# One pool of eight PSUM banks for every product, and the order of all steps rewritten

## The chip, the cores and the metric

The kernel runs on one core of a Trainium2 chip. The metric is the device time of one execution in microseconds (us). Shown are the median of three timed executions and one profiled execution.

## The reference, cut to what matters

Two layers follow each other. The first is causal attention with a decay bias (8 batches, 8 heads, 576 positions, head size 64), the second a mixture of 4 attention experts over the first one's output, with 2 experts chosen for each position.

```python
def _attn_ref(q, k, v, s):                      # (8, 8, 576, 64), s (8, 8, 576)
    scores = scale * np.matmul(q, k.transpose(0, 1, 3, 2))
    cum = np.cumsum(np.maximum(s, 0.0), axis=-1)
    bias = -(cum[:, :, :, None] - cum[:, :, None, :])
    scores = np.where(causal, -1e9, scores + np.minimum(bias, 0.0))
    scores = scores - np.max(scores, axis=-1, keepdims=True)
    attn = np.exp(scores)
    attn = attn / (np.sum(attn, axis=-1, keepdims=True) + 1e-09)
    return np.matmul(attn, v)

def _moe_ref(x, w_gate, wq, wk, wv, wo):        # x (8, 576, 512), 4 experts of 64
    logits = x @ w_gate                         # the two largest are kept and softmaxed: w
    for e in range(E):
        q, k, v = x @ wq[e], x @ wk[e], x @ wv[e]
        # causal softmax attention a of this expert
        ye = a @ v @ wo[e]
        # out += w of expert e (zero where it is not chosen) * ye
```

## The kernel before

The work is cut into pairs: two heads of one batch, or two experts of one batch, are one pair, worked on side by side. There are 50 slots, one for each pair and two without. In the steady part six slots make up one batch: four pairs of heads (phase 1) of batch b and then two pairs of experts (phase 2) of batch b-1. The list of `MIDDLE` that holds for a slot is named by its phase and its number in the batch, (1,0) to (1,3) and then (2,0) and (2,1).

Slot n works on pair n and, ahead or behind, on its neighbours. A step is a closure with a short name, and these are the names that matter here (the slot in which a step stands in the order is written before a colon, `0:s2`):

- `ld`: load of queries and keys of pair n+3 (L357, a DMA on SyncE's queue). `lv`: the values (L367, L368). `hc`: the rows with the running sums (L394 to L401).
- `h0` to `h3` (ACT, L406, L409): high parts of queries and keys of pair n+2. `lq`, `lk`: copies of the high parts for pair n+1 (GpSimd or ACT at the start, DMAs later). `l0` to `l3` (DVE, L441, L446): low parts.
- `m0` to `m5` (TensorE, L466): scores in bf16 for the row maxima, one bank each; m3 to m5 are of pair n+1, m0 to m2 of pair n+2. `M0` to `M5` (DVE, L480): the maximum out of the bank. `cb` (DVE, L499) joins two parts. `mt` (TensorE, L503) transposes the maxima, `mA` (ACT, L507) copies them out, `mq` (DMA, L511) writes them into row 96 of the query tile, where the scores product subtracts them.
- `s0` to `s6` (TensorE, L529, L534): scores of pair n, one bank each; `E0` to `E6` (ACT, L550, L560): exponentials. `d0` to `d3` (GpSimd): causal masks and column sums.
- `v0` to `v7` (TensorE, L625): attention times values of pair n-1, in two banks; `V0`, `V1` (ACT, L639): their copies.
- `a0`, `a1` (TensorE, L675) and `A0`, `A1` (ACT): sums over positions; `r0` to `r4`: their reciprocals, spread through memory by DMAs; `n`, `N`, `o`: normalisation and the split into high and low parts.
- `p`, `P` (TensorE L840, ACT L858, L875, L1000): projections of the second layer and their copies. `t0`, `t1`: transposed gate weights. At the end `x..`, `y..`, `q..`, `z..` finish the last pair, the last output projection and its stores.

TensorE's products are of two kinds by the columns of the array that they take. Scores and projections take it whole (weights of 128 columns, or 64 for a last short tile). The products m and v come as two halves of 64 columns, a as four strips of 32.

The order of the whole program is written out in lists: `FILLING` for slots -2 to 9, `MIDDLE` for slots 10 to 43 (six lists, used again and again), `DRAINING` for 44 to 49. Each engine executes its own instructions in the order in which the lists name them, and SyncE issues the DMAs in that order; between engines semaphores make a step wait for what it reads and for the buffer that it writes. A step listed earlier on another engine delays nobody, a step listed earlier on the same engine does.

PSUM has eight banks, and before the change each belongs to a kind of product: two for m (`mx0`, `mx1`), three for s (`s0` to `s2`, by turns), one for v (`pvp`), and two (`pj0`, `pj1`, by turns, `bank_pj`) for all others. At the very end the output projection borrows `mx0`, `mx1` and `s0`. A product waits until its own kind's bank has been read.

Of the kernel before, what the change touches and what calls it, by code (L numbers as in the profile page):

```python
# [8 lines left out]
F32 = mybir.dt.float32  # L9
# [30 lines left out]
def pieces(kt, q0, q1):  # L40
# [4 lines left out]
    for ci, segs in enumerate(SCHUNKS):  # L45
# [65 lines left out]
    ),  # L111
# [4 lines left out]
    ),  # L116
# [4 lines left out]
    ),  # L121
# [4 lines left out]
    ),  # L126
# [4 lines left out]
    ),  # L131
# [1011 lines left out]
```

## Time and profile before

| | |
|---|---|
| median of 3 timed executions | 699.51 us (697.83 to 701.18) |
| profiled execution, its own time | 699.62 us |
| its span, first to last instruction | 697.9 us |
| TensorE busy | 660.4 us, 95% of the span |
| VectorE (DVE) busy | 559.6 us, 80% |
| ScalarE (ACT) busy | 460.2 us, 66% |
| GpSimd (POOL) busy | 459.8 us, 66% |
| mean granted TensorE clock | 0.994 |

Each row of a busy time is the time in which the engine had at least one instruction under way. Matmuls overlap, so a busy TensorE is not one at its peak: what a product really costs is read from the distance between the start of one matmul and that of the next.

### The profile page before, as it was taken

Reading aid. Unit: us, or ns where it says so; the run is one execution under the profiler, and the core shown is the slowest. Engines: PE = TensorE matmul, PEld = TensorE weight load, DVE = VectorE, ACT = ScalarE, POOL = GpSimd, SP = SyncE. Lnnn points to the kernel's source line nnn. Section 1 sums busy time; section 2 is a strip of 40 time slices with the busy share of each in tenths; the row PEclk is TensorE's granted clock in tenths of the full one; section 3 lists DMA queues with packets and bytes.
Section 4 is the critical chain, followed back from the end, with each engine's and each line's share of the span. In section 5 each row is a group of like instructions: output and inputs, shape, how many; then the busy total and the mean of one; then the engine's idle time right before and its main releaser. Section 6 shows DMA issues by size and latency. Waiting matters only on the chain.

```text
span 697.9 us, 16217 instructions
## 1 busy us (share of the span) xinstructions
PE 660.4 (95%) x5816; PEld 526.4 (75%) x5816; DVE 559.6 (80%) x1478; ACT 460.2 (66%) x971; POOL 459.8 (66%) x611
## 2 busy tenths in 40 slices
PE   1587999999999999999999999999999999999997
PEld 0364578878877788878977878878877788879775
DVE  5588996889889888898779878888789887762983
ACT  6276868676657756767766766776676776566463
POOL 9595677578776568666777667766776578736120
PEclk9999999999999999999999999999999999999999
DMA  3433442445355533566444542655534553431304
GB/s 111 128 95 109 135 126 63 121 123 105 104 129 160 159 92 84 143 182 127 109 121 129 150 123 71 172 141 136 123 81 142 159 123 103 107 98 37 85 9 137
DMA packets 52158, 81.21 MB, mean 116 GB/s; under 512 B 18430, under 2 KB 26622, under 8 KB 52078
## 3 DMA queue, kind: packets, MB, share of 16 engines
q1 hardware_dynamic: 52078, 80.18, 43.9%
q8 instruction: 46, 0.75, 0.4%
q14 instruction: 34, 0.28, 0.1%
HBM read 44.55 MB, written 10.09 MB: 78 GB/s over the span
## 4 chain that ended last, share of the span: by engine, by line
PE 73%; DVE 10%; DMA 7%; ACT 4%; issue 3%; SPq 2%; POOL 1%; DVEq 0%; ACTq 0%; POOLq 0%
PE pq L840 13%; PE pvp L625 13%; PE s L529 10%; PE s L534 9%; PE mx L466 8%; PE po L840 7%; PE pw L840 6%; DVE mx L480 4%; PE sm L675 3%; DMA rb<-rr 2%; ACT p L550 1%; DMA rr<-sr 1%; DVE k L446 1%; PE mt L503 1%; DVE q L441 1%
## 5 line engine op out<-in xcount | busy, mean ns | idle before, releaser
L480 DVE CUSTOM_DVE_ANT_0 mx<-mx,mask 128x512 f32<-128x512 f32 (+7 forms) x480 | 217.7, 469 | 56.9 <-PE mx L466 48.5
L569 POOL TENSOR_SCALAR_AFFINE_SELECT p<-p 128x256 f32<-128x256 f32 (+1 forms) x240 | 124.9, 521 | 136.0 <-ACT p L550 135.5
L550 ACT ACTIVATE p<-s 128x512 f32<-128x512 f32 x288 | 163.8, 588 | 58.9 <-PE s L534 55.7
L529 PE MATMUL s<-q,k 128*128 128x256 f32 (+3 forms) x672 | 177.2, 290 | 1.4 <-ACT p L550 1.2
L534 PE MATMUL s<-q,k 97*128 97x256 f32 (+3 forms) x672 | 163.2, 285 | 4.6 <-DMA q<-mr 4.4
L529 PEld LDWEIGHTS s<-q,k 128*128 128x128 f32 (+1 forms) x672 | 124.2, 185 | 20.9 <-issue 12.6
L591 POOL TENSOR_TENSOR r<-r,p 128x640 f32<-128x640 f32 x92 | 133.3, 1448 | 7.7
L534 PEld LDWEIGHTS s<-q,k 97*128 97x128 f32 (+1 forms) x672 | 123.8, 186 | 7.6 <-DMA q<-mr 6.1
L466 PE MATMUL mx<-k,q 96*64 96x320 bf16 (+7 forms) x960 | 107.1, 303 | 23.1 <-ACT q L406 12.5
L625 PE MATMUL pvp<-p,v 128*64 128x128 f32 (+4 forms) x1024 | 105.1, 338 | 0.5 <-ACT pv L639 0.4
L441 DVE TENSOR_TENSOR q<-raw,q 64x576 fp32r<-64x576 f32 x94 | 84.0, 898 | 13.8 <-ACT q L406 8.6
L446 DVE TENSOR_TENSOR k<-raw,k 64x576 fp32r<-64x576 f32 x94 | 80.5, 865 | 16.3 <-DMA k<-k 14.1
L625 PEld LDWEIGHTS pvp<-p,v 128*64 128x64 f32 x1024 | 66.5, 137 | 29.9 <-issue 2.6
L466 PEld LDWEIGHTS <-q 96*64 96x64 bf16 x960 | 45.9, 111 | 56.7 <-DVE mcol L480 18.3
L840 PE MATMUL pq<-xh,wqkh 128*128 128x288 f32 x256 | 77.1, 301 | 0.0
L840 PE MATMUL pq<-xl,wqkh 128*128 128x288 f32 x256 | 75.7, 296 | 0.2 <-DVE xl L739 0.2
L840 PE MATMUL pq<-xh,wqkl 128*128 128x288 f32 x256 | 75.4, 295 | 0.0
L586 POOL TENSOR_TENSOR r<-p 128x256 f32<-128x256 f32 x46 | 41.3, 897 | 50.9 <-ACT p L550 41.3
L409 ACT ACTIVATE k<-raw 64x576 fp32r<-64x576 f32 x96 | 63.9, 680 | 4.5 <-DMA raw<-in_qk_dram 3.0
L406 ACT ACTIVATE q<-raw 64x576 fp32r<-64x576 f32 x96 | 64.5, 680 | 1.9 <-PE s L534 0.7
L480 DVE DVE_READ_ACCUMULATOR2_ANT mcol<- 128x1 f32 x480 | 63.8, 133 | 1.4
L639 ACT ACTIVATE pv<-pvp 128x256 f32<-128x256 f32 x92 | 37.3, 405 | 39.5 <-PE pvp L625 39.3
(117 smaller groups left out, 1181.8 us busy)
## 6 DMA issues: line engine op xcount, KB each, us to landing
raw<-in_qk_dram SPq DMA_DIRECT2D x30, 576.0 KB
rb<-rr SPq DMA_DIRECT2D x92, 144.0 KB
q<-q SPq DMA_DIRECT2D x45, 288.0 KB
k<-k SPq DMA_DIRECT2D x39, 288.0 KB
v<-in_vm_dram SPq DMA_DIRECT2D x32, 256.0 KB
out_dram<-o SPq DMA_DIRECT2D x32, 256.0 KB
q<-mr SPq DMA_DIRECT2D x96, 2.2 KB
raw<-in_qk_dram SPq DMA_DIRECT2D x4, 288.0 KB
```

The lines of the kernel that those rows point to most:

```text
L406: nc.scalar.activation(q2[0:64, j], get_raw(n, j)[0:64], AF.Copy)
L441: eng.tensor_tensor(a[64:128, j], get_raw(n, j)[0:64], q2[0:64, j].bitcast(F32), op=OP.subtract)
L446: eng.tensor_tensor(c[0:64, j], get_raw(n, j)[64:128], c[64:128, j].bitcast(F32), op=OP.subtract)
L466: nc.tensor.matmul(t[64 * j : 64 * j + 64, c0 : c0 + k1 - k0], q2[0:RC, 64 * qt : 64 * qt + 64], k2[0:RC, k0:k1], start=True, stop=True,)
L480: nc.vector.tensor_tensor_reduce(t[:, c0 : c0 + w], t[:, c0 : c0 + w], mask[:, m0 : m0 + w], scale=1.0, scalar=NEG, op0=OP.add, op1=OP.max ...
L529: nc.tensor.matmul(t[0:nk, c0 : c0 + q1 - q0], K1[r1(n)][:, j, k0 : k0 + nk], Q1[r1(n)][:, j, q0:q1], start=True, stop=False,)
L534: nc.tensor.matmul(t[0:nk, c0 : c0 + q1 - q0], K2[r2(n)][0 : RM + 1, j, k0 : k0 + nk], Q2[r2(n)][0 : RM + 1, j, q0:q1], start=False, stop= ...
L550: nc.scalar.activation(ptile[n][:, x % 2, 512 * ci : 512 * ci + 512], tl[x], AF.Exp, scale=0.125)
L569: nc.gpsimd.affine_select(out=a, in_=a, pattern=[[0, 2], [1, nk]], compare_op=OP.is_ge, fill=0.0, base=0, channel_multiplier=-1,)
L591: add(r[:, :, q0:S], r[:, :, q0:S], p[:, :, 1024 + c : 1024 + c + S - q0], op=OP.add)
L625: nc.tensor.matmul(cur[h][64 * j : 64 * j + 64, q0 - PVC[h] : q1 - PVC[h]], vsl(j, kt), ptile[n][:, j, c : c + q1 - q0], start=first, stop ...
L840: nc.tensor.matmul(t[0:nk, 0:w], l, r, start=(x == 0), stop=(x == len(terms) - 1))
```

## The change

All eight banks go into one queue. `take` hands out the bank at the head of the queue, `give` puts a bank back at its tail when the step that reads it out is listed. Both happen while the program is written, so the lists decide which bank a product gets; on the chip the product waits, as before, until the bank's last reader is done. A bank's last reader is now sometimes ACT and sometimes DVE.

```diff
+    banks = list(range(8))
+    taken = {}
+
+    def take(name):
+        t = ps.tile([P, 512], F32, tag=f"bank{banks[0]}", name=name, bufs=1)
+        taken[id(t)] = t, banks.pop(0)
+        return t
+
+    def give(t):
+        banks.append(taken.pop(id(t))[1])
...
-            mbank[n, bi] = t = ps.tile([P, 512], F32, tag=f"mx{bi % 2}", name=f"mx{n}_{bi}", bufs=1)
+            mbank[n, bi] = t = take(f"mx{n}_{bi}")
...
-            return ps.tile([P, 512], F32, tag=f"s{(x + n) % 3}", name=f"s{n}_{x}", bufs=1)
+            return take(f"s{n}_{x}")
...
-                cur[h] = ps.tile([P, 512], F32, tag="pvp", name=f"pvp{n}_{h}", bufs=1)
+                cur[h] = take(f"pvp{n}_{h}")
...
-        t = bank_pj(name)
+        t = take(name)
...
+                give(t[0])
```

Each copy or reduction that reads a product out ends with a `give` of its bank, and every `bank_pj` becomes a `take`. No instruction is added, removed or resized. All lists are new. Every step keeps its slot and stands elsewhere in the order; the list of slots (1,0), as an example:

```diff
-        "l2 v0 lk m3 v1 M3 s0 hc E0 p0 s2 ld s3 s1 V0 h1 E1 E2 h0 lq h2 P0 p1 s4 s5 l1 m4 M4 E4 "
-        "v2 m5 M5 v3 v4 h3 m2 v5 M2 v6 m1 E3 d1 v7 m0 cb mt P1 mA l3 M1 lv d0 p2 s6 a1 P2 V1 mq "
-        "E5 M0 d2 l0 a0 A0 A1 E6 d3"
+        "v0 m3 v1 s1 s0 l2 hc lq h2 E1 E0 s3 s2 ld p0 P0 p1 s5 h0 M3 E3 V0 h3 m5 M5 h1 m4 M4 v2 "
+        "v4 m2 v3 v5 m0 cb P1 E2 E5 mt p2 s4 M2 mA l0 s6 a0 lv E6 lk l1 mq E4 a1 m1 P2 d1 A1 d2 "
+        "d3 d0 l3 A0 M1 M0 v6 v7 V1"
```

The stretch of `FILLING` up to the first scores, from where the two orders part on SyncE's queue (`...` stands for steps left out; `0:ld` waits until a buffer of pair 0 has been read):

```diff
-    "-1:hc -1:m0 0:ld -1:M3 0:lv -1:mt -1:l0 -1:M0 0:h1 -1:l2 -1:m2 -1:mA -1:m1 0:h2 -1:mq 0:s2 "
...
+    "0:l1 0:l0 -1:hc -1:m2 -1:mA 0:l3 -1:m0 0:m5 -1:mq -1:m1 -1:cu 0:h2 0:h3 -1:l0 -1:l3 -1:l2 "
+    "-1:l1 0:s2 0:s1 -1:M0 0:s3 0:E3 0:s0 0:ld 0:E0 0:m4 -1:M2 0:m3 0:M5 0:lc 0:l2 0:E1 0:M4 "
```

In the new list `-1:ld` and `-1:hc` follow `1:lv` on SyncE's queue, and `0:lv` comes after `0:mq`; on GpSimd `0:lq` comes after `0:lc` and `0:f2`, and on ACT `-1:lk` after the four steps `-2:h`.

More of the change, by code (lines that the diff above doesn't have):

```diff
@@ L484, in reduce @@
                 )
+            give(t)
         for bi in banks:
@@ L501, in turn @@
         def turn():
-            t[0] = bank_pj(f"mt{n}")
+            t[0] = take(f"mt{n}")
             nc.tensor.transpose(t[0][0:9, 0:P], mcol[n][:, 0:9], ident)
@@ L552, in exp @@
             )
+            give(tl[x])
         def tail():
@@ L563, in exp_tail @@
             )
+            give(tl[6])
         def diag(kt):
@@ L639, in copy @@
                 nc.scalar.activation(pvtile[n][:, q], cur[h][:, 0:w], AF.Copy)
+            give(cur[h])
         x = 0
@@ L670, in half @@
         def half(h):
-            t[h] = bank_pj(f"sm{n}_{h}")
+            t[h] = take(f"sm{n}_{h}")
             for x in range(2):
@@ L686, in copy @@
             )
+            give(t[h])
         return {
@@ L751, in sum_up @@
             q0, q1 = LASTQ[k]
-            t[k] = bank_pj(f"sm{m}_{k}")
+            t[k] = take(f"sm{m}_{k}")
             for j in range(2):
@@ L765, in copy @@
             )
+            give(t[k])
         def one_over(k):
@@ L790, in tile_attention_then_moe @@
     ot = {}
-    npj = [0]
-    def bank_pj(name):
-        npj[0] += 1
-        return ps.tile([P, 512], F32, tag=f"pj{npj[0] % 2}", name=name, bufs=1)
     def out_tile(b, tt):
@@ L809, in part @@
             if tt not in t:
-                t[tt] = (
-                    bank_pj(f"po{b}_{tt}") if tt < 2 else
-                    ps.tile([P, 512], F32, tag=("mx0", "mx1", "s0")[tt - 2], name=f"po{b}_{tt}", bufs=1)
-                )
+                t[tt] = take(f"po{b}_{tt}")
             for x, (y, w) in enumerate(((xH, WOH), (xH, WOL), (xL, WOH))):
@@ L822, in copy @@
             nc.scalar.activation(out_tile(b, tt)[0:nk, 0:DM], t[tt][0:nk, 0:DM], AF.Copy)
+            give(t[tt])
         def store(tt):
@@ L858, in copy @@
                 nc.scalar.activation(raw2[b, e // 2][:, e % 2, q], t[0][:, 0:HS], AF.Copy)
+                give(t[0])
             return mm, copy, None
@@ L875, in copy @@
                 nc.scalar.activation(vx[0:nk, tt, :], t[0][0:nk, 0:260], AF.Copy)
+                give(t[0])
             return mm, copy, None
@@ L927, in turn @@
             o, tts = parts[x]
-            t[x] = bank_pj(f"gt{b}_{o}")
+            t[x] = take(f"gt{b}_{o}")
             for tt in tts:
@@ L939, in copy @@
             nc.scalar.activation(t["g4"][:, o : o + w], t[x][0:E, 0:w], AF.Copy)
+            give(t[x])
         def send():
@@ L957, in spread @@
         def spread(i, h):
-            t["k", i, h] = bank_pj(f"gt{b}{i}_{h}")
+            t["k", i, h] = take(f"gt{b}{i}_{h}")
             nc.tensor.matmul(
@@ L969, in keep @@
             )
+            give(t["k", i, h])
         items = {
@@ L1000, in copy @@
                 nc.scalar.activation(t[1][0:nk, 0:DM], t[0][0:nk, 0:DM], AF.Copy)
+                give(t[0])
             def store():
```

159 rows, old and new, of tables (DRAINING, FILLING, MIDDLE) are left out of this document.

## The prediction

> **What bounds the kernel now.** I read the page first: busy times, then the slices.
>
> ```profile
> span 697.9 us, 16217 instructions
> PE 660.4 (95%) x5816; PEld 526.4 (75%) x5816; DVE 559.6 (80%) x1478; ACT 460.2 (66%) x971; POOL 459.8 (66%) x611
> PE   1587999999999999999999999999999999999997
> PEclk9999999999999999999999999999999999999999
> ```
>
> TensorE is busy from the fourth slice to the last but one; only the first 60 us show holes. The profiled execution took 699.62 us, 1.7 us around its span and 0.1 us above the median of 699.51, so terms of the span carry over to the time unchanged. Next, busy times by stretch (TensorE, weight loads, DVE, ACT, POOL, clock, DMA): three of the start, then one full batch of the steady part, from the first scores of slot 17 to those of slot 23.
>
> ```profile
> 20.00:40.00 20.00, 12.60 (x77) 8.94 (x75) 11.32 (x40) 8.29 (x17) 11.92 (x15) 0.95 0.44 127
> 40.00:60.00 20.00, 16.49 (x138) 10.53 (x136) 16.25 (x40) 15.71 (x32) 16.28 (x22) 0.96 0.34 90
> 80.00:100.00 20.00, 19.15 (x169) 12.54 (x168) 18.33 (x48) 16.12 (x32) 10.17 (x15) 1.00 0.38 108
> 249.80:329.71 79.91, 79.26 (x729) 64.79 (x725) 67.94 (x181) 54.73 (x118) 55.24 (x73) 1.00 0.52 129
> ```
>
> In the steady batch TensorE is busy 79.26 of 79.91 us, DVE 67.94, the others about 55. So TensorE's own sequence sets the pace, and DVE has 12 us of room. At the start nobody is full: 7.4 us of TensorE are empty between 20 and 40 us, 3.5 between 40 and 60. What it waits for there is in the waits of TensorE (us in total, times, longest); the last row is the same question for 100 to 680 us alone.
>
> ```profile
> PE mx L466 <- DVE mcol L480: 9.2, 13, 1.8
> PE s L534 <- DMA q<-mr: 4.4, 1, 4.4
> PE mt L503 <- DVE mcol L499: 2.6, 10, 0.3
> PE s L529 <- ACT p L550: 1.2, 3, 0.8
> ...
> PE mt L503 <- DVE mcol L499: 2.3, 9, 0.3
> ```
>
> The row of 9.2 us is bank waiting (m waits until DVE has read its bank), and since it is absent after 100 us, all of it lies in the start. Last, the timeline, because a busy TensorE hides what one product costs. Start, duration, instruction:
>
> ```profile
> 234.91 0.40 PE L466 MATMUL mx<-k,q 96*64 96x512 bf16 x2
> 235.13 0.39 PE L625 MATMUL pvp<-p,vx 128*64 128x128 f32 x4
> ...
> 269.08 0.22 PE L529 MATMUL s<-q,k 128*64 128x64 f32 x1
> 269.14 0.22 PE L534 MATMUL s<-q,k 97*64 97x64 f32 x1
> 269.29 0.42 PE L466 MATMUL mx<-k,q 96*64 96x512 bf16 x2
> 269.54 0.71 PE L625 MATMUL pvp<-p,v 128*64 128x256 f32 x6
> ...
> 275.49 0.39 PE L466 MATMUL mx<-k,q 96*64 96x512 bf16 x2
> 275.81 0.39 PE L529 MATMUL s<-q,k 128*128 128x256 f32 x1
> 276.03 0.28 PE L534 MATMUL s<-q,k 97*128 97x256 f32 x1
> 276.15 0.28 PE L529 MATMUL s<-q,k 128*128 128x256 f32 x1
> ```
>
> The same step m3 (two matmuls of 512) lasts 0.22 us between half-array products (234.91 to 235.13), 0.25 when it comes from scores (269.29 to 269.54), 0.32 when scores follow (275.49 to 275.81). The small scores matmul before it takes 0.15 instead of 0.06 us (269.14 to 269.29, after 269.08 to 269.14), and the first scores matmul after it 0.22 instead of 0.12 (275.81, 276.03, 276.15). So leaving a grouping of columns costs 0.10 us in either direction, arriving at the whole array 0.10 more, arriving at halves 0.03. No wait is shown for it; it is inside the busy time.
>
> **The change part by part.**
>
> **1. Switches on TensorE.** The new lists hold the same 1277 TensorE steps. Counted in the lists, neighbouring steps of different grouping (whole, halves, strips) go from 286 to 222, 64 fewer: 44 fewer in the middle (30 to 22 per batch), 15 in the end, 5 in the start. Of these arrivals at the whole array fall from 117 to 97, at halves from 127 to 92. That is 64 x 0.10 + 20 x 0.10 + 35 x 0.03 = 6.4 + 2.0 + 1.1 = 9.5 us. All of it lies on the path where TensorE is full, which holds for middle and end. I take -9.5. Bounds: -11 if arrivals at halves cost 0.07; -7 if those of the tiny transposes t (14 of the 64) and of the start are free.
>
> The Trainium skill, TensorEngine Tiling (Array Packing), Key Properties, says that a change of tiling mode, not of tile, drains the engine; the rows agree that there is a price. The Trainium skill's page TensorE: Matmul & The Clock Gate, Step-by-step, puts the drain at about 128 cycles, at 2.4 GHz an estimate of 0.053 us, and by it 64 switches would be worth 3.4 us, and the sum below would end at 687. The rows show twice that in one direction and four times in the other, so they decide.
>
> **2. The first scores.** This fence holds the start, SPq being SyncE's queue.
>
> ```profile
> 11.97 0.41 SPq L357 DMA_DIRECT2D raw<-in_qk_dram  x1
> 13.91 0.70 DVE L480 CUSTOM_DVE_ANT_0 mx<-mx,mask 128x512 f32<-128x512 f32 x1 [2.89 <-PE mx L466]
> 14.70 0.84 DVE L446 TENSOR_TENSOR k<-raw,k 64x576 fp32r<-64x576 f32 x1
> 16.03 1.25 ACT L409 ACTIVATE k<-raw 64x576 fp32r<-64x576 f32 x2 [2.96 <-DMA raw<-in_qk_dram]
> 19.00 0.73 DVE L480 CUSTOM_DVE_ANT_0 mx<-mx,mask 128x512 f32<-128x512 f32 x1
> 20.48 0.27 ACT L507 ACTIVATE mr<-mt 9x128 fp32r<-9x128 f32 x1 [3.19 <-PE mt L503]
> 22.48 0.38 SPq L357 DMA_DIRECT2D raw<-in_qk_dram  x1
> 22.91 0.46 SPq L367 DMA_DIRECT2D v<-in_vm_dram  x1
> 23.41 0.72 SPq L368 DMA_DIRECT2D v<-in_vt_dram  x1
> 24.23 1.57 SPq L511 DMA_DIRECT2D q<-mr  x2
> 27.65 0.64 PE L534 MATMUL s<-q,k 97*128 97x320 f32 x1 [4.42 <-DMA q<-mr]
> ```
>
> The maxima of pair 0 are copied out at 20.75 (`mA`), but `mq` is issued at 24.23: in SyncE's queue it stands behind `0:ld`, which could not go before 22.48, and `0:lv`. The scores start 3.42 us after the issue, at 27.65. In the new list `mq` stands ahead of both. What is late next: DVE reads pair 0's six banks in 13.91 to 19.73 without the low part of 14.70 (0.84), so 5.0 us; the new order starts with m1, some 0.3 later, and ends near 19.2, followed by `mt`. ACT comes to `mA` after `0:h0`, which needs `-1:ld`. That DMA is now behind the two issues of `1:lv` (0.46 + 0.72 us by the same two of `0:lv` at 22.91 and 23.41), so from 13.2; by 11.97 to 16.03 it is usable at 17.2, and three copies of 0.63 (1.25 for two) end at 19.1, later if the values' transfer shares its engines. `mA` ends between 19.6 and 20.8, the scores start 3.5 later, 23.1 to 24.3; the four low parts on DVE (0.84 each) end at 22.6 and are not last. Gain 3.4 to 4.5; I take -3.5, bounds -4.4 (the wait's row) and 0.
>
> Of the other moves at the start: `0:lq` behind `0:lc` and `0:f2` on POOL, and `0:lv` behind `0:mq` and a weight load on SyncE, are needed by pair 1's scores and v only, 10 us later; hidden, and worth up to +2 us if POOL's list (11.92 of 20 us busy) slips. `-1:lk` after `-2:h` on ACT serves the first product, which waits for the running sums anyway: nothing.
>
> **3. Bank waits at the start.** One row of the 9.2 us:
>
> ```profile
> 60.32 0.33 PE L466 MATMUL mx<-k,q 96*64 96x256 bf16 x4 [1.83 <-DVE mcol L480]
> ```
>
> With eight banks m need not wait for the reduction two products back. Counted in the new lists, from slot 5 on, the time in TensorE steps between the last product into a bank and the next into it is under 1.1 us for 5 of 892 products (43 before), never under 0.77 (0.46 before). But the start is short of DVE too (16.25 and 18.33 of 20 us above), and a bank not waited for leaves the maxima themselves, needed by `mt`, as late as DVE makes them. I give it a third of the 9.2: -3, bounds 0 and -9.
>
> **4. Waits of the steady part.** In each batch two `mt` stall and one m behind a v:
>
> ```profile
> 271.71 0.87 DVE L499 TENSOR_TENSOR mcol<-mcol 128x1 f32<-128x1 f32 x1
> 272.12 0.28 PE L534 MATMUL s<-q,k 97*128 97x192 f32 x1
> 272.73 0.27 PE L503 MATMUL mt<-ident,mcol 128*9 128x128 f32 x1 [0.33 <-DVE mcol L499]
> ```
>
> The matmul at 272.12 should be followed after 0.11 to 0.12; it is 0.61, so 0.48 us wait, of which the row's 0.33 is the visible part. By the distances of starts, waits of 0.12 us or more add up to 8.6 us between 100 and 680 us (29 of them; 1.3 per batch). The new lists put 2.2 to 7.5 us of TensorE work between the last m of a pair and its `mt` (1.2 to 3.1 before), and 4.2 to 6.7 between `mt` and the first scores (2.8 to 6.4). I take half of 8.6: -4.5, bounds 0 and -8.6.
>
> **5. New waits.** A FIFO of banks makes TensorE wait for the reader listed first, though another bank may be free already; m now takes banks that ACT reads, where a copy stands behind exponentials.
>
> ```profile
> L550 ACT ACTIVATE p<-s 128x512 f32<-128x512 f32 x288 | 163.8, 588 | 58.9 <-PE s L534 55.7
> L639 ACT ACTIVATE pv<-pvp 128x256 f32<-128x256 f32 x92 | 37.3, 405 | 39.5 <-PE pvp L625 39.3
> ```
>
> A copy of 0.41 behind one exponential of 0.59 takes 1.0 us, against a shortest lead of 0.77: a quarter of a microsecond, in the handful of products under 1.1 us. A faster TensorE also leaves DVE less room: 67.94 of some 77.5 us a batch, 88%, with `r1` in slot (2,1) now waiting on DVE for its DMA with a low part behind it, which nobody needs before the next slot. I add +2; bounds 0 and +8.
>
> Sum: -9.5 - 3.5 - 3 - 4.5 + 2 = -18.5. From 699.6 that is **681 us**. The tail after the last matmul is not touched: the last copy and store stand as before.
>
> **The rivals.**
>
> *The maxima on DVE take over in the middle.* TensorE's steps get shorter, but `cb`, 0.87 us in the row above for a single column, comes as late as before, and `mt` and scores wait for it. Then the middle keeps its 79.9 us per batch: lost are 44 of the 64 switches (6.9 us) and term 4, and the time is 681 + 6.9 + 4.5 = 692. For it speaks DVE's 85%; against it the 12 us of room and the longer leads of term 4.
>
> *The start does not move.* If another chain (DVE, the sums' DMA) ends last there, terms 2 and 3 go: 681 + 6.5 = 687.5. For it: 18.33 of 20 us of DVE by 80 us. Against: between 20 and 40 us every engine has 8 us free.
>
> *All waits go.* Terms 3 to 5 at their better half: 671.
>
> *Slower: banks behind ACT.* The mechanism of term 5 at every m: if each of its 249 products from slot 5 on waits 0.1 us for ACT, that is 25 us, 706. It decides from about 0.08 us per m. Against it: s already gets all its banks back from ACT, and its row shows 1.2 us in three waits.
>
> *Slower: the clock falls back.* In the window 20 to 40 us the clock's mean is 0.95, while TensorE stands idle for 7.4 us; in the steady batch with waits under 0.6 us it is 1.00. If the round of eight banks split the work with idle times long enough for a lower clock, each 20 us with the loss of that window (5% of 12.6 us, 0.6) would cost 0.6 us, over 33 such windows 20: 701. The Trainium skill, TensorE: Matmul & The Clock Gate, A second HAM failure mode, describes such a swing between clocks where products cycle through the banks; this trace shows no sign of it while TensorE is fed.
>
> *It does nothing.* If the price of a switch is one of the order of operands and not of the grouping, and waits only move, 699.
>
> **How the numbers follow.** Forecast 681 (675 to 687): 0.45. The start does not move, 687.5: 0.20. DVE takes over, 692: 0.18. All waits go, 671: 0.10. Banks behind ACT, 706: 0.04; clock 701: 0.01; nothing, 699: 0.02. The range from 668 to 694 leaves out the last three (0.07) and the edges of 692 and 671, some 0.1 together. Within 0.5% is 696 to 703, about what a measurement can tell from no change: 0.03 from nothing and clock; slower 0.04; faster 0.93.
>
> **What would show it.** Switches: a steady batch of 77 to 78.5 us instead of 79.91 at an equal count of matmuls, and scores following scores. First scores: `mq` issued right after `mA`, the first L534 before 25 us. Banks: the row mx <- DVE of 9.2 us under 6. `mt`: its 2.3 us in the middle under 1. New waits: rows of TensorE waiting for ACT's L639, L858 or L550. The prediction is wrong if a batch stays near 79.9 us (then DVE's or POOL's rows end TensorE's idle time), or if the switches' 0.10 us turn out to belong to waits.

## The result and the profile after

The changed kernel takes 680.01 us (median of four executions, 676.58 to 681.32) against 700.28 us (697.83 to 701.18) of the kernel before, run beside it: a ratio of 0.9708 (95% interval 0.9664 to 0.9753). Forecast were 681 us, 668 to 694. The profiled execution took 679.88 us with a span of 677.8. The page after, as it was read before:

```profile
span 677.8 us, 16340 instructions
PE 645.1 (95%) x5816; PEld 532.1 (79%) x5816; DVE 550.7 (81%) x1478; ACT 451.9 (67%) x971; POOL 449.1 (66%) x611
PE   1689899999999999999999999999999999999997
PEclk9999799999999999999999999999999999999989
```

The same 5816 matmuls keep TensorE busy 15.3 us less (660.4 before), and the slices of the start are a little fuller. The second view is the stretches of the start and two full batches, each from the first scores of slot 17 (23) to those of slot 23 (29); columns as before: length, TensorE, weight loads, DVE, ACT, POOL, clock, DMA.

```profile
20.00:40.00 20.00, 15.49 (x122) 11.95 (x120) 17.59 (x52) 13.86 (x27) 14.46 (x19) 1.00 0.43 121
40.00:60.00 20.00, 18.43 (x162) 11.67 (x156) 17.73 (x51) 14.03 (x28) 18.23 (x24) 0.91 0.48 127
240.51:320.02 79.51, 78.37 (x727) 65.66 (x726) 65.94 (x181) 53.80 (x117) 54.85 (x73) 1.00 0.49 130
320.02:398.25 78.23, 77.71 (x727) 65.27 (x726) 66.82 (x181) 53.95 (x117) 54.93 (x73) 1.00 0.50 132
```

A batch takes 78.23 us where it took 79.91, and TensorE is busy 77.71 of it instead of 79.26. (The batch of 79.51 holds a stall near 304 us that the next batch, of the same lists, does not have; a second trace of this kernel, shown at the end, has 78.55 there.) In the start TensorE works 15.49 and 18.43 us of two stretches instead of 12.60 and 16.49, and DVE 17.59 of the first instead of 11.32: DVE is nearly full (17.6 to 18.0 of each 20 us) from 20 to 80 us. The waits of TensorE, the last three rows for 100 to 680 us alone:

```profile
PE mt L516 <- DVE mcol L492: 6.7, 5, 3.6
PE mx L478 <- DMA k<-cum: 2.5, 2, 2.1
PE s L543 <- DVE k L458: 1.1, 1, 1.1
PE s L548 <- DMA q<-mr: 1.0, 2, 0.7
PE mx L478 <- ACT p L564: 0.9, 1, 0.9
PE mx L478 <- DVE mcol L492: 0.9, 1, 0.9
...
PE mt L516 <- DVE mcol L492: 0.7, 1, 0.7
PE s L548 <- DMA q<-mr: 0.7, 1, 0.7
PE mt L516 <- DVE mcol L512: 0.3, 1, 0.3
```

The bank wait of m for DVE fell from 9.2 us to 0.9, and the scores' wait for `mq` from 4.4 to 1.0. In their place `mt` waits 6.7 us for the maxima (L492), 6.0 of them in the start, and m once 2.1 us for the running sums. The timeline of the first scores:

```profile
19.28 0.37 PE L516 MATMUL mt<-ident,mcol 128*9 128x128 f32 x1 [3.65 <-DVE mcol L492]
19.69 0.27 ACT L520 ACTIVATE mr<-mt 9x128 fp32r<-9x128 f32 x1 [0.40 <-PE mt L516]
19.98 1.53 SPq L525 DMA_DIRECT2D q<-mr  x2
22.40 0.39 SPq L369 DMA_DIRECT2D raw<-in_qk_dram  x1
22.49 0.61 PE L543 MATMUL s<-q,k 128*128 128x320 f32 x1 [1.15 <-DVE k L458]
22.89 0.47 PE L548 MATMUL s<-q,k 97*128 97x320 f32 x1
```

`mq` goes out right behind `mA` at 19.98, ahead of `0:ld` (22.40), and the first L548 stands at 22.89 instead of 27.65.

Where the 20.1 us of span went is read from four marks: the first matmul, the first of slot 10, the first of slot 44, and the last. Rows of before, then of after (the start of the one-row group at 145.60 lies just ahead of slot 10, whose first v begins at 146.04):

```profile
12.49 0.60 PE L466 MATMUL mx<-k,q 96*64 96x512 bf16 x1 [12.49 <-ACT q L406]
153.76 0.43 PE L625 MATMUL pvp<-p,vx 128*64 128x256 f32 x2
608.45 0.31 PE L466 MATMUL mx<-k,q 96*64 96x256 bf16 x4
693.09 0.40 PE L815 MATMUL po<-woh,xl 128*64 128x512 f32 x1
```

```profile
12.29 0.37 PE L478 MATMUL mx<-k,q 96*64 96x256 bf16 x1 [12.29 <-DMA k<-p]
145.60 0.83 PE L641 MATMUL pvp<-p,vx 128*64 128x192 f32 x10
590.50 0.28 PE L478 MATMUL mx<-k,q 96*64 96x256 bf16 x2
673.37 0.40 PE L825 MATMUL po<-woh,xl 128*64 128x512 f32 x1
```

The start is 7.7 us shorter (153.76 to 146.04), the middle 10.2 (454.7 to 444.5), the end 1.8 (84.6 to 82.9), and what follows the last matmul 0.4. The second trace of the changed kernel has 443.2 us in the middle, without the stall near 304 us, and 81.2 in the end, where the one above lost 1.7 us to a lower clock (last section). The kernel before has the full clock there, so at an equal clock the end is 3.4 us shorter.

To part the middle into switches and waits I took for each step the distance to the next step's start, over six traces, grouped by kind and shape of step and by the groupings of its two neighbours; the lower third of each group is the step without waiting. Summed along the order of slots 10 to 43 this gives 443.4 us before and 436.4 after; the rest of the measured stretch, 11.3 and 8.1 us, is waiting. So switches gave 7.0 us and waits 3.2. The split is an estimate: it moves by about 1 us with the way in which steps are grouped.

### The profile page after: what moved, and what is told of

The parts are those of the page before. It is cut to its first block, busy times and chain, and to the rows that moved or that the text cites. A ratio compares the mean times of both kernels' runs of the same rounds, so it can differ in the third digit from the quotient of the medians.

```text
span 677.8 us, 16340 instructions
## 1 busy us (share of the span) xinstructions
PE 645.1 (95%) x5816; PEld 532.1 (79%) x5816; DVE 550.7 (81%) x1478; ACT 451.9 (67%) x971; POOL 449.1 (66%) x611
## 4 chain that ended last, share of the span: by engine, by line
PE 81%; DVE 6%; DMA 5%; ACT 3%; issue 2%; SPq 2%; POOL 1%; DVEq 0%; ACTq 0%; POOLq 0%
PE pvp L641 16%; PE pq L851 15%; PE s L543 10%; PE s L548 10%; PE mx L478 9%; PE pw L851 8%; PE po L851 6%; PE sm L692 3%; DVE mx L492 2%; DMA k<-cum 2%; DMA rb<-rr 1%; PE mt L516 1%; PE po L825 1%; ACT p L564 1%; DVE k L458 1%
## 5 line engine op out<-in xcount | busy, mean ns | idle before, releaser
L492 DVE CUSTOM_DVE_ANT_0 mx<-mx,mask 128x512 f32<-128x512 f32 (+5 forms) x480 | 217.3, 471 | 52.7 <-PE mx L478 35.1
L564 ACT ACTIVATE p<-s 128x512 f32<-128x512 f32 x288 | 159.6, 588 | 61.2 <-PE s L548 53.1
L543 PE MATMUL s<-q,k 128*128 128x320 f32 (+3 forms) x672 | 172.2, 286 | 2.0 <-DVE k L458 1.1
L548 PE MATMUL s<-q,k 97*128 97x320 f32 (+3 forms) x672 | 160.4, 284 | 1.0 <-DMA q<-mr 1.0
L607 POOL TENSOR_TENSOR r<-r,p 128x640 f32<-128x640 f32 x92 | 129.6, 1409 | 7.7
L548 PEld LDWEIGHTS s<-q,k 97*128 97x128 f32 (+1 forms) x672 | 123.6, 185 | 3.2 <-DMA q<-mr 1.8
L478 PE MATMUL mx<-k,q 96*64 96x384 bf16 (+6 forms) x960 | 96.4, 303 | 17.2 <-DMA k<-p 12.7
L641 PE MATMUL pvp<-p,v 128*64 128x128 f32 (+4 forms) x1024 | 100.1, 337 | 0.4 <-ACT p L564 0.4
L453 DVE TENSOR_TENSOR q<-raw,q 64x576 fp32r<-64x576 f32 x94 | 82.8, 882 | 14.9 <-ACT q L418 12.4
L641 PEld LDWEIGHTS pvp<-p,v 128*64 128x64 f32 x1024 | 69.8, 138 | 20.5 <-issue 1.9
L492 DVE DVE_READ_ACCUMULATOR2_ANT mcol<- 128x1 f32 x480 | 65.5, 137 | 0.9
L655 ACT ACTIVATE pv<-pvp 128x256 f32<-128x256 f32 (+1 forms) x92 | 36.2, 406 | 38.0 <-PE pvp L641 38.0
L751 DVE TENSOR_TENSOR pv<-pv,rb 128x576 f32<-128x576 f32 x46 | 40.6, 889 | 23.0 <-DMA rb<-rr 22.4
```

What stands on the lines that cost most here:

```text
L453: eng.tensor_tensor(a[64:128, j], get_raw(n, j)[0:64], q2[0:64, j].bitcast(F32), op=OP.subtract)
L478: nc.tensor.matmul(t[64 * j : 64 * j + 64, c0 : c0 + k1 - k0], q2[0:RC, 64 * qt : 64 * qt + 64], k2[0:RC, k0:k1], start=True, stop=True,)
L492: nc.vector.tensor_tensor_reduce(t[:, c0 : c0 + w], t[:, c0 : c0 + w], mask[:, m0 : m0 + w], scale=1.0, scalar=NEG, op0=OP.add, op1=OP.max ...
L543: nc.tensor.matmul(t[0:nk, c0 : c0 + q1 - q0], K1[r1(n)][:, j, k0 : k0 + nk], Q1[r1(n)][:, j, q0:q1], start=True, stop=False,)
L548: nc.tensor.matmul(t[0:nk, c0 : c0 + q1 - q0], K2[r2(n)][0 : RM + 1, j, k0 : k0 + nk], Q2[r2(n)][0 : RM + 1, j, q0:q1], start=False, stop= ...
L564: nc.scalar.activation(ptile[n][:, x % 2, 512 * ci : 512 * ci + 512], tl[x], AF.Exp, scale=0.125)
```

## The experiments

The theory: the gain has three sources, fewer switches on TensorE (0.16 us each), the first scores' `mq`, and fewer waits; the pool by itself gives only waits back. The rivals: the pool is what gains, whatever the order; or a switch costs less (0.053 us, the lower price in the prediction), and the batch is shorter for another reason. The kernel before, run between these, had medians of 700.3 to 700.7 us.

**The pool with the old order.** The changed kernel's `take` and `give`, all lists as before (286 switches):

```diff
-FILLING, MIDDLE, DRAINING: new
+FILLING, MIDDLE, DRAINING: as before
```

> The new bank rule with all of the old lists, so 286 switches of grouping as before. Theory (the new order makes most of the gain, the pool alone only takes away bank waits): the waits of m for DVE's read of its bank shrink at the start (9.2 us before) and partly come back as waits for the maxima, and in the middle the waits of m behind a v (0.27 us a batch) go; 3 to 5 us faster than before, 695 to 697 us. Rival (the freedom of the banks is the gain): 686 us or less.

Measured: 713.86 us, ratio to before 1.0194 (1.0165 to 1.0222). Neither theory had that: the pool alone makes the kernel 13 us slower. It is not the clock: executions with a mean granted clock of 0.982 and 0.994 took 713.94 and 713.78 us. In the start the pool does take the bank waits of m away, 9.2 us before and 0.5 now, but others come in their place, and slot 10 begins at 155.3 us instead of 153.8. Three rows of TensorE's waits of 0 to 100 us, then the first three of 160 to 640 us:

```profile
PE s L548 <- DMA q<-mr: 7.8, 2, 5.9
PE mt L516 <- DVE mcol L492: 3.0, 1, 3.0
PE mx L478 <- DVE mcol L492: 0.5, 1, 0.5
```

```profile
PE pvp L641 <- DVE mcol L492: 6.0, 12, 1.6
PE mt L516 <- DVE mcol L512: 4.2, 10, 0.6
PE s L543 <- issue: 3.5, 1, 3.5
```

v never waited for DVE before, having a bank that only ACT reads. One of the twelve, in slot 19:

```profile
292.76 1.27 DVE L453 TENSOR_TENSOR q<-raw,q 64x576 fp32r<-64x576 f32 x1
293.95 0.61 DVE L492 CUSTOM_DVE_ANT_0 mx<-mx,mask 128x448 f32<-128x448 f32 x1
294.70 0.23 DVE L492 CUSTOM_DVE_ANT_0 mx<-mx,mask 128x64 f32<-128x64 f32 x1
294.85 0.14 DVE L492 DVE_READ_ACCUMULATOR2_ANT mcol<- 128x1 f32 x1
295.14 1.08 PE L641 MATMUL pvp<-p,v 128*64 128x320 f32 x8 [0.53 <-DVE mcol L492]
```

The queue hands v the bank of m0. Its reduction stands on DVE behind a low part of 1.27 us and is done at 294.99; by the starts and ends in the trace that is 3.7 us after m0 itself. By the steps between, v wants the bank some 3.1 us after m0, and stands still for 0.5. In the kernel before the same reduction came 2.9 us late too, but only a later m waited for that bank.

**Whose banks?** Two cuts of that kernel: v keeps a bank of its own (pool of seven), or m keeps its two (pool of six).

```diff
...
-                cur[h] = take(f"pvp{n}_{h}")
+                cur[h] = ps.tile([P, 512], F32, tag="pvp", name=f"pvp{n}_{h}", bufs=1)
...
```

> The pool under the old lists (713.9 us) once more, but v has a bank of its own and the pool is of seven. Theory: what the pool costs under the old lists is that a product gets a bank whose reader is DVE, who is late; the row of v waiting for DVE (6.0 us in 12 waits over 0.25 us between 160 and 640 us, more in shorter ones) goes, but mt and s still take such banks: 704 to 708 us. Rival: the loss lies elsewhere (in the waits of mt for the joined maxima, or in the doubled kinds of semaphores): 711 to 714.

```diff
...
-            mbank[n, bi] = t = take(f"mx{n}_{bi}")
+            mbank[n, bi] = t = ps.tile([P, 512], F32, tag=f"mx{bi % 2}", name=f"mx{n}_{bi}", bufs=1)
...
```

> The pool under the old lists (713.9 us) once more, but m, the only product read by DVE before its bank is given back, keeps its two banks mx0 and mx1, and the pool is of the six others. Theory: no product read by ACT waits for DVE's banks any longer, so the middle falls back to the batches of before, 79.9 us, and the time to 697 to 701. Rival: coupling between the readers is not the cause; then m gets fewer banks than in the pool and the time stays at 711 or rises.

Measured: 705.19 us (ratio 1.0074, 1.0046 to 1.0102) and 698.99 us (0.9979, 0.9961 to 0.9998), both inside the theory's ranges. Waits of 160 to 640 us, all that the second one has left:

```profile
PE mt L515 <- DVE mcol L511: 3.3, 12, 0.3
```

So the loss is the coupling of two kinds of readers: with m's banks kept apart, sharing the six others is worth 0.2% (at most 0.4), and the 13 us are gone. In the start, too, the rows are those of before again (m waits 8.7 us for DVE).

**The lists one by one.** Old `MIDDLE` lists in the changed kernel (266 switches), then the old `FILLING` (227).

> The changed kernel with the six old lists for slots 10 to 43; pool, start and end stay new. 266 switches, 44 more than the changed kernel. Theory: 6.9 us of switches and some 3 us of waits for the maxima come back, a batch takes 79.4 to 79.9 us again: 689 to 690 us. Rival (in the middle the pool did it): 682 us or less, a batch near 78.2 us.

> The changed kernel with the old list FILLING (slots -2 to 9), the other lists new: 227 switches instead of 222. Theory: the order of the start is worth what it showed between the two kernels, 7.8 us up to slot 10, and a little more, since the old lists under the pool reached slot 10 at 155.3 us and the changed kernel at 146.0: about 688 to 690 us, slot 10 at 154 to 156, and a middle and end as in the changed kernel. Rival: the eight banks alone shorten the start and its order only moves waits: below 683.

Measured: 697.96 us (ratio 0.9970, 0.9947 to 0.9993) and 692.8 us (0.9889, 0.9863 to 0.9915), 18 and 13 us above the changed kernel; expected were 9 to 10 and 8 to 10. In the first the batches take 81 us, 1 us more than before the change, since the old lists meet the new bank rule (v waits for DVE 4.9 us, `mt` for the joined maxima 4.9). In the second slot 10 starts at 156.1 us, 10 later than in the changed kernel, and the first batch has one more stall:

```profile
159.58 0.14 DVE L492 DVE_READ_ACCUMULATOR2_ANT mcol<- 128x1 f32 x1
159.82 0.36 PE L543 MATMUL s<-q,k 128*128 128x256 f32 x1 [2.67 <-issue]
```

The profile names no releaser. But in the order of `take` and `give` these scores get the bank of the m0 of slot 9, whose reduction DVE ends at 159.72, and they begin 0.1 us later. With the pool under the old lists the stall stands at the same place (3.46 us), again with scores in that bank and 0.1 us behind its reduction. So it is the same coupling. From the pool alone (713.9 us) to the changed kernel the new lists are worth 34 us, all under the pool: 13 for `FILLING`, 18 for `MIDDLE`, and some 3 that were not run apart, for `DRAINING` or for the parts together.

**The price of a switch.** In the changed kernel one scores step of each middle list is moved into a run of half-array products: 290 switches for 222, no step added. For slots (1,0), for instance, s5 goes behind m4's reduction:

```diff
...
-p1 s5 h0 M3 E3 V0 h3 m5 M5 h1 m4 M4 v2 v4
+p1 h0 M3 E3 V0 h3 m5 M5 h1 m4 M4 s5 v2 v4
...
```

> The changed kernel with one scores step in each of the six middle lists moved a few products later, into the middle of a run of half-array products: 68 more switches (34 arrivals at the whole array, 34 at halves), everything else as it is. Theory (0.10 us to leave a grouping, 0.10 more to arrive at the whole array, 0.03 at halves): 6.8 + 3.4 + 1.0 = 11 us slower than the changed kernel, 691 us. The page's drain of 0.053 us: 3.6 us, 684 us. Rival (the price belongs to waits, not to the grouping): 680 to 682 us.

Measured: 693.73 us (690.75 to 697.63), 13.7 above the changed kernel; the spans differ by 13.9. One batch:

```profile
326.42:407.25 80.83, 80.09 (x727) 65.13 (x726) 65.77 (x181) 54.21 (x117) 54.01 (x73) 1.00 0.47 128
```

2.6 us more than 78.23, and 2.4 of it inside TensorE's busy time. By the sums over steps, 11.5 us are price (447.9 instead of 436.4, that is 0.17 us for each of 68) and 1.5 new waits (9.6 instead of 8.1). Expected were 11 us. The rival of 0.053 us a switch would have given 684, that of waits 682 at most, and both fall.

**The first scores, both ways.** `0:ld` back ahead of `mq` in the changed kernel, and `0:ld`, `0:lv` behind `mq` in the kernel before:

```diff
-... -1:mA 0:l3 -1:m0 0:m5 -1:mq ... 0:s0 0:ld 0:E0
+... -1:mA 0:l3 -1:m0 0:m5 0:ld -1:mq ... 0:s0 0:E0
```

> The changed kernel with one step moved back: 0:ld stands ahead of -1:mq on SyncE's queue, as in the old order. Theory (the first scores wait for mq and the start is one chain): mq is issued near 22.8 instead of 20.0 us, the first scores start near 26 instead of 22.5, and the whole is 3 to 4 us slower than the changed kernel, 683 to 684 us. Rival (DVE's work at the start absorbs it): within 1 us, 680 to 681 us.

```diff
--1:m0 0:ld -1:M3 0:lv -1:mt ... 0:h2 -1:mq 0:s2
+-1:m0 -1:M3 -1:mt ... 0:h2 -1:mq 0:ld 0:lv 0:s2
```

> The kernel before with its own banks and lists, only the two loads 0:ld and 0:lv moved behind -1:mq. Theory: the wait of 4.4 us of the first scores goes and the start is shorter by the 3.9 us that the reverse edit cost the changed kernel, at least by 3.5: 696 to 697. Rival: with two banks for m, DVE's bank waits take over at once and less than 1.5 us is left: 699 to 700.

Measured: 683.95 us (682.88 to 685.53), 3.9 above the changed kernel, and 696.36 us (ratio 0.9930, 0.9906 to 0.9955), 4.2 below the kernel before. The place of `mq` in SyncE's queue is worth 4 us with either way of dealing out banks.

**Another rule under the new lists.** Of the free banks m takes the oldest that DVE gave back, and every other product the oldest that ACT gave back:

```diff
+        by = "M" if name.startswith("mx") else "other"
+        at = next((x for x, b in enumerate(banks) if b[1] == by), 0)
+        bank = banks.pop(at)[0]
...
```

> The changed kernel with all its lists, but of the free banks m takes the oldest one that DVE gave back and every other product the oldest one that ACT gave back, and any other only if there is none. By the lists, products with less than 1.1 us of TensorE steps since their bank's last product then number 81 instead of 5 (34 of them m), and products on a bank of the other kind 99 instead of 396. Theory (the reader's lateness counts, the lists are made for the oldest bank): the short distances turn into waits of some 0.1 to 0.2 us each, 8 to 16 us: 688 to 696. Rival (coupling of the readers is the only price): fewer crossings, 680 or less.

Measured: 724.2 us (ratio 1.0329, 1.0292 to 1.0365), 44 above the changed kernel with the same order and the same 222 switches. The rival falls; the theory has the sign, and its size (8 to 16 us) is some three to five times too small. Waits and one batch:

```profile
PE mx L481 <- DVE mcol L495: 27.4, 37, 1.4
```

```profile
259.39:342.92 83.53, 79.14 (x728) 65.47 (x727) 66.50 (x181) 54.35 (x117) 53.06 (x73) 1.00 0.47 124
```

The waits in that row are of 0.74 us on average, not of 0.1 to 0.2: a bank of m comes back only behind DVE's other work. In the new order of the changed kernel 80 of the 204 reductions of slots 10 to 43 end more than 2.5 us after their product, the latest 8.4 us; before the change it was 44, and 6.4. The new lists let DVE be later, and the round through eight banks leaves room for it; that last step is argued from these counts.

**The wait that came up.** `4:hc`, whose DMA m awaits for 2.1 us at 77 us in the changed kernel, listed ahead of `5:w0`:

```diff
-5:l2 5:w0 3:d3 ... 4:E1 4:hc 5:m4
+5:l2 4:hc 5:w0 3:d3 ... 4:E1 5:m4
```

> The changed kernel with the DMA that writes the running sums of slot 4 (4:hc) listed one load of slot 3 to 5 earlier, ahead of 5:w0. In the changed kernel a product m waits 2.14 us for it at 77 us, with DMAs queued ahead of it on SyncE. Theory: the wait goes and the time falls by 1 to 2 us, to about 678.5. Rival: the maxima on DVE are as late there as TensorE, so that the wait turns into another and nothing changes: 680, ratio to the changed kernel within 0.1%.

> The kernel with 4:hc ahead of 5:w0 once more, beside the changed kernel on the same chip. Theory: the removed wait of 2.1 us is worth 1 to 2 us, so 678 to 679. Rival: its earlier median of 676.8 against 680.0 was spread between executions and the two agree within 0.7 us.

> The changed kernel unaltered, for a comparison with the next one on the same chip. All theories: 680 us, 678.5 to 681.5.

Measured: 676.78 us (675.98 to 681.29; ratio to before 0.9677, 0.9649 to 0.9706), then on one chip 678.32 (677.41 to 680.41) beside 679.63 (676.57 to 682.69) of the changed kernel. The row with the 2.1 us (2.5 in all) falls to 0.5. The medians are 1 to 3 us lower, but the executions of both spread over more than that, and in the two profiled ones with the move slot 10 begins later than without it, at 148.5 and 148.1 us against 146.0 and 145.7. Whether it gains anything stays open.

## Why the prediction was right, point by point

- **Switches, -9.5 (bounds -11 and -7): right in mechanism and size.** Of the 44 in the middle, 6.9 us were expected, and 7.0 are found there; the end, with 15 fewer, gave 1.8, and 3.4 at an equal clock, where waits are not taken apart. The price per switch in the middle was 0.16 by the prediction and is 0.17 in the run with 68 more. The Trainium skill, TensorEngine Tiling (Array Packing), Key Properties, says that a change of mode drains the engine: the trace agrees that it has a price. That price is about three times the 0.053 us that the prediction estimated from the Trainium skill, TensorE: Matmul & The Clock Gate, Step-by-step. A batch of 78.23 us lies in the 77 to 78.5 that was named.
- **First scores, -3.5 (bounds -4.4 and 0): right, somewhat low.** 4.8 us at the spot, 3.9 to 4.2 carried through to the end. `mA` ended at 19.96, in the range given; the first L548 came at 22.89, just before it. The low parts were called not last, ending at 22.6: they end at 22.34, and TensorE, idle for 1.15 us, waits for them last.
- **Bank waits at the start, -3 (bounds 0 and -9): the size fits, the cause does not.** m's row falls by 8.3 us, and `mt` gets 6.0 in the start for the maxima themselves, as the step said. 7.7 us of the start less the 4.8 of the first scores leave 2.9 for this step, for the five switches there and for the 0.2 us by which the first matmul is earlier. But the step gave its 3 us to the eight banks. The pool under the old lists takes m's row away just so (0.5 us) and reaches slot 10 1.5 us later than before. What the start gained beyond `mq` came only together with its new order.
- **Steady waits, -4.5, and new waits, +2: the net of -2.5 was nearly met, by a wrong test.** The waits of the middle fell by 3.2 net, and by 4.5 in the second trace. They were larger than the 8.6 us that the step counted: 11.3 by the sums over steps. But both terms, and the rival "banks behind ACT", rested on a distance: 1.1 us of TensorE steps between two products in one bank was held to be enough. The pool under the old lists has 2 such products (the scores of the 3.46 us are one) and loses 13 us; v waits there for banks last used 2.0 and 3.1 us before. The test holds for a bank read by ACT (m waited once for it, 0.9 us) and not for one read by DVE, which ends four reductions in ten of the new order over 2.5 us after the product. The rival on the slower side named the wrong engine: not m behind ACT, but v, `mt` and once the scores behind DVE.
- **The sum.** 681 was forecast, 680.0 measured. What the prediction did not see is that the two halves of the change cannot be added: it priced the order and the pool each by itself, the pool as a net gain of about 1 us (-3 and +2). Without the new lists it costs 13, and with the new lists another rule for the free bank costs 44. So it was luck that the number came out right: nothing in the sum asked whether lists and rule fit each other, and these two do.
- **The rivals.** That the start does not move and that DVE takes over in the middle are both refuted by rows above; DVE has 66.8 us of the 78.2 of a batch, 85% as before. The clock does not fall back in the middle: 1.00 in every stretch of 20 us from 100 to 640 us, so the swing that the Trainium skill, TensorE: Matmul & The Clock Gate, A second HAM failure mode, describes for products cycling through banks does not show there. The rival's reading of the trace before was wrong, though: it put the 0.95 of 20 to 40 us down to idle time, and TensorE is busy throughout the 3.41 us (38.1 to 41.5) in which the clock was at half there. The 671 us of "all waits go" do not follow from the terms, whose better bounds give 669.

Not tried is the new order with the old banks. It can't stand: at 279 places of the new lists a product would take its kind's bank before the step that reads the last product is listed, and up to five banks of m and five of s are held at once. Whether an order with few switches exists for fixed banks stays open, and with it how much of the 7.0 us needs the pool.

## What to carry to other kernels

A common queue of buffers ties every user to the slowest reader listed before it, so judge it by how late each reader is (end of the read after the product, from the trace), not by the distance between two uses on the producer. Change the sharing of a buffer and the order of steps together, or keep apart the buffers of the engine that runs late: here the first is worth 20 us, the second loses nothing and gains 0.2%, and the pool with an order not made for it is 13 us the wrong way. When TensorE is busy throughout, look for the price inside the busy time: one matmul in three surroundings gave a price per switch that held to about a tenth in the middle.

## What was not expected of the hardware

The granted clock falls to one half for stretches of 3.41 us, or a few times that, in the first 100 us of every trace here and in some of them later. In the four below TensorE is busy throughout. The execution of 679.88 us of the changed kernel has three; columns as before, and last the row that ends just ahead of the third:

```profile
50.11:53.52 3.41, 3.41 (x25) 1.25 (x26) 3.27 (x10) 2.59 (x7) 3.33 (x5) 0.50 0.46 97
77.42:84.25 6.83, 6.83 (x42) 4.73 (x40) 5.18 (x19) 5.08 (x11) 6.07 (x9) 0.50 0.33 94
654.27:657.68 3.41, 3.41 (x23) 2.46 (x24) 2.85 (x5) 1.65 (x6) 1.26 (x4) 0.50 0.15 54
652.15 2.20 PE L973 MATMUL gt<-g,sel 4*128 4x288 f32 x8
```

The execution of 676.63 us has one. Below it stand its batch from slot 17 on, its first matmul of slot 44 and its last matmul:

```profile
37.53:40.93 3.40, 3.40 (x19) 2.19 (x21) 3.20 (x4) 3.35 (x8) 2.32 (x4) 0.50 0.23 49
239.84:318.39 78.55, 77.86 (x727) 65.59 (x726) 66.96 (x181) 53.84 (x117) 55.44 (x73) 1.00 0.50 132
588.88 0.54 PE L478 MATMUL mx<-k,q 96*64 96x256 bf16 x6
670.10 0.40 PE L825 MATMUL po<-woh,xl 128*64 128x512 f32 x1
```

What such a stretch costs depends on where it falls. In the end, where TensorE sets the pace, 82.9 us stand against 81.2: 1.7 us, the half of 3.41. Of the eight traces with the new `DRAINING` and the queue of eight banks, the five with a stretch there have 82.8 to 83.0 us in the end and the three without it 81.2 to 81.3. In the start the first execution loses 5.1 us of clock and the second 1.7, and yet they reach slot 10 at 146.0 and 145.7 us. So of the 3.25 us between these two the stretch at the end makes 1.7, the stall near 304 us 1.3, and the start 0.3. The spread between executions is not the clock's alone: two executions of the changed kernel with a mean clock of 0.997 took 676.63 and 682.69 us.

What sets the stretches off is not shown. With `4:hc` moved, the 2.1 us wait at 77 us was gone, and the clock between 80 and 100 us was still 0.91. In all five traces that have the late stretch, it begins in the last of the four products of the row L973 or at most 1.1 us behind them; they use 4 rows of the array, for 2.2 us. In the 24 us ahead of each of the five, TensorE is busy without a gap. The kernel before has these products in two pairs with other work between, and no stretch there. But four traces have the new sequence without a stretch, so that it is the cause is a guess.
